# A list scheduler inside a kernel gets a corrected table of durations, and its small VectorE copies become bitwise or operations

## The chip, the cores and the metric

The kernel runs on one core of a Trainium2 chip. The metric is the device time of one launch in microseconds (us). A core has TensorE (matmuls, results in PSUM), VectorE, ScalarE, GpSimd and SyncE (it issues most DMAs), each with an instruction queue of its own that runs in order. In the profile they are PE (with PEld for the loading of weights), DVE, ACT, POOL and SP.

## The reference

A gated linear attention is followed by a Fourier mixing over tokens and features and by a feed-forward block, for 4 batches, 8 heads of 48 features, and 768 tokens (all float32):

```python
for t in range(S):
    state = alpha[:, :, t, :, None] * state + np.einsum('bhd,bhe->bhde', k[:, :, t], v[:, :, t])
    y[:, :, t] = np.einsum('bhd,bhde->bhe', q[:, :, t], state)
...
X = np.fft.fft(np.fft.fft(x, axis=1), axis=2)      # x: y as [4, 768, 384]
u = x + np.real(X)
un = (u - mean(u)) / np.sqrt(var(u) + 1e-06)
out = u + np.maximum(un @ w_ch1, 0.0) @ w_ch2      # 384 -> 1536 -> 384
```

## The kernel before

Heads are taken in pairs (112 partitions), so each batch has four pairs, 16 in all. For one pair, `products` makes the running products of the decays: two VectorE scans over 768 steps (tiles `w` and `al`, with a helper row `d`), and around them small copies of every 64th element. Products of k and q with these (`times`, on VectorE or GpSimd) give operands of TensorE; the score blocks are evacuated from PSUM by ScalarE and masked by GpSimd (`affine_select`); a short scan per head (`tt`, 288 elements) carries the state between blocks of 128 steps. From the eighth pair on the scores are made from split operands (`qs`). `combine` adds and subtracts the two halves of the sequence (tiles `sd`, mostly on GpSimd). `mix_stages` then folds the features (`f2`, VectorE, with three small copies for each of three tiles), multiplies by cosine and sine tables, and adds the result to `y`. `norm_stages` normalises, and `ffn_stages` runs the feed-forward block for each of two blocks of 384 tokens: 12 tiles of the hidden layer, each with 9 matmuls in and 9 out, because weights and activations are kept as a high and a low part. Between the two, ScalarE and VectorE make the high and low part of `h`. The weights arrive as float64 and are taken apart in `wsplit`, in the first part of the run.

None of this is emitted in program order. Every instruction is written down in a `Plan` with a key (a priority: numbers such as `KW`, `KN`, `KA`), the tiles it touches and an estimate of its duration (`duration`). `emit` then goes through time as it estimates it: it keeps a clock for every engine, asks which instructions have all their operands, takes the one with the lowest key among those that could start within a short window, gives it a tile, and advances the clock of its engine. The order so found is the order of the instructions in each engine's queue, DMA issues on SyncE and GpSimd included. Where an instruction may run on one of two engines (`FX`: `'VG'` is VectorE or GpSimd), this is where the engine is chosen:

```python
done = max(now, t) + op.durs[e] - SLACK[e]
if any(max(clock[o], start(op, o)) + op.durs[o] < done for o in op.engines if o != e):
    continue
```

The feed-forward block of one batch has a late key, so that it fills TensorE's time beside the attention of the next batch. The first 120 us of the plan get small matmuls on a tile of zeros wherever the plan sees TensorE idle (`WARM`). Since all instructions are emitted from `emit` (line 434), nearly all rows of the profile name that line; they are told apart by their tiles.

Of the kernel before, what the change touches and what calls it, by code (L numbers as in the profile page):

```python
# [112 lines left out]


class View:
    """A tile of the plan, or a part of one: the steps are replayed on the real tile."""

    def __init__(self, tile, steps=()):
        self.tile, self.steps = tile, steps
# [14 lines left out]


class Slot:
    """One tile as the program sees it; it gets a real tile of its tag when its first instruction is placed."""

    def __init__(self, tag, real=None):
        self.tag, self.real, self.uses, self.touched, self.access, self.last = tag, real, 0, [], [], None  # L140
# [1 line left out]


class Rows:
    """Row numbers of an indirect DMA."""

    def __init__(self, view):
        self.view = view
# [25 lines left out]


class Plan:
    """Instructions written down in program order, then given an order on every engine by list scheduling."""

    def __init__(self, engines):
        self.engines, self.ops, self.tags, self.direct, self.key, self.chain, self.fill = engines, [], {}, None, 0.0, None, False  # L180
# [35 lines left out]
    def add(self, engines, name, args, kwargs):  # L216
        engine = engines[0]
        fns = {e: self.method(e, name) for e in engines}
        if self.direct:
            return fns[engine](*[real(a) for a in args], **{k: real(x) for k, x in kwargs.items()})  # L220
        op = Op(engines, fns, args, kwargs, self.key)
        n = len(self.ops)
        self.ops.append(op)
        named = [("out" if i == 0 and "out" not in kwargs else i, a) for i, a in enumerate(args)] + list(kwargs.items())
        op.free, op.fill = 1, self.fill
        op.bytes = None
        for k, a in named:
            if isinstance(a, Rows):
                a = a.view
            if isinstance(a, View):  # L230
                self.touch(n, op, a, k in ("out", "accum_out"))
                if k == "out":
                    op.free = self.region(a)[4]
                if k == 2:
                    op.moving = a
        op.name = name
        named = dict((str(k), a) for k, a in named)
        op.durs = {e: self.duration(op, named, e) for e in engines}
        if engine == "SP" and isinstance(named["out"], View):
            if self.chain is not None and self.chain not in op.deps:  # L240
                op.behind = self.chain
                op.deps.add(self.chain)
            self.chain = n
        if "dma" in name:
            op.wire = self.wire(named)
# [43 lines left out]
    def duration(self, op, named, engine):  # L289
        n = op.free  # L290
        if "dma" in op.name:
            return 1.05 if engine == "POOL" else 0.05
        if engine == "PE":
            m = self.region(named["1"])[4]
            if op.name == "transpose":
                return max(m, self.region(named["2"])[4]) / 1200 + 0.002
            if str(named["1"].real(self.base(named["1"])).dtype).endswith("float32"):
                return max(m, n) / 600 + 0.004
            return n / 2400 + 0.003
        if engine == "ACT":  # L300
            pointer = 0.094 if any(isinstance(named.get(k), View) for k in ("bias", "scale")) else 0.0
            return (0.05 if self.psum(named.get("1")) else 0.093) + n / 1200 + pointer + (0.096 if "accum_out" in named else 0.0)
        if op.name == "memset":
            return n / (960 if engine == "DVE" else 1100) + 0.01
        if engine == "DVE":
            if op.name == "bn_stats":
                return 0.47
            if op.name == "reciprocal":
                return 0.07 + n / 160
            if isinstance(named.get("scalar1"), View):  # L310
                return 0.07 + n / 1200
            whole = "bitcast" in [s[0] for s in named.get("out", View(None)).steps]
            pointer = 0.06 if isinstance(named.get("scalar"), View) else 0.0
            return 0.07 + pointer + n / (1920 if whole and op.name == "tensor_scalar" else 960)
        return 0.126 + n / 1094 if op.name == "affine_select" else 0.15 + n / 477

    def psum(self, view):
        return isinstance(view, View) and view.tile.tag in ("a", "f1", "f2")
# [12 lines left out]
    def emit(self):  # L331
# [10 lines left out]
                    wait[e].append(n)  # L342
        dge, wire = 0.0, 0.0
        order = []

        def start(op, e):
            t = op.ready[e]
# [13 lines left out]
        while placed < len(ops):  # L361
# [38 lines left out]
                    order.append(self.idle[0])  # L400
            if op.name == "matmul" and self.idle and (op.args[0].tile.tag, op.args[0].tile.cell) == self.idle[3]:
                self.open = not op.kwargs["stop"]
            end = t + op.dur
            clock[op.engine] = end
            if "dma" in op.name:
# [38 lines left out]


SLACK = {'ACT': 2.0, 'DVE': 0.5, 'POOL': 5.0}
FX = {'comb': 'G', 'mul': 'VG', 'first': 'G', 'wm': 'VG', 'wd': 'VG', 'fold': 'V', 'ev': 'A', 'relu': 'A', 'un': 'V', 'hi': 'A', 'xh': 'A', 'er': 'AV', 'fc': 'V', 'kl': 'V'}
WINDOW = {'PE': 0.0, 'ACT': 0.15, 'DVE': 0.05, 'POOL': 0.5, 'SP': 0.0, 'DMA': 0.0}


# [1 line left out]
def gla_mix_ffn(ctx: ExitStack, tc: tile.TileContext, alpha, kq, v, w1, w2, consts, rowtab, out):  # L452
# [41 lines left out]
    def w3():  # L494
        return plan.tile("w3")

    def fixed(shape, name, dtype=F32):
        return plan.fixed(cp.tile(shape, dtype, name=name))

# [1 line left out]
    cst = fixed([P, CONST_W], "cst")  # L501
    ident = cst[:, ID_O : ID_O + P]
    wts = [None] * (NW // 2)
# [101 lines left out]
        FL["hi"].copy(hi, a2)  # L605
        FL["wd"].tensor_sub(lo, a2, hi.bitcast(F32))

# [1 line left out]
    def attn_stages(b, hp, i, mixed):  # L609
        tt, mt = tts[i], mts[hp % 3]  # L610
        pair = b * NP2 + hp
# [3 lines left out]
        def products(lo, hi):  # L615
            as_, Af, o = loaded["al", pair], e["A"], off(lo)
            d, chunks = d1[0:CW, lo:hi], slice(lo // C, hi // C)
            V.tensor_copy(d[:, 0::C], as_[0:CW, o : o + hi - lo : C])
            V.memset(as_[0:CW, o : o + hi - lo + 1 : C], 0.0)
            part = Af[0:CW, lo:hi]  # L620
            V.tensor_tensor_scan(out=part, data0=as_[0:CW, o : o + hi - lo], data1=d, initial=0.0, op0=ALU.mult, op1=ALU.add)
            V.memset(d[:, 0::C], 0.0)
            V.memset(d[:, C - 1 :: 2 * C], 1.0)
            r = rec[0:CW, chunks]
            V.reciprocal(r, part[:, C - 1 :: C])
            V.tensor_copy(d[:, 2 * C - 1 :: 2 * C], r[:, 1::2])
            j0, j1 = max(lo // P - 1, 0), hi // P - 1
            V.tensor_mul(mt[0:CW, j0:j1], Af[0:CW, j0 * P + P - 1 : j1 * P : P], Af[0:CW, j0 * P + P + C - 1 : j1 * P + C : P])
            V.tensor_tensor_scan(
                out=as_[0:CW, o + hi - lo : o : -1], data0=as_[0:CW, o + hi - lo : o : -1], data1=d[:, ::-1],  # L630
                initial=0.0, op0=ALU.mult, op1=ALU.add,
            )
            V.memset(d[:, C - 1 :: C], 0.0)
            first = part.rearrange(halves, h=2, t=C)[:, :, 0]
            FL["first"].tensor_mul(first, first, r[:, 0::2, None].broadcast_to([CW, (hi - lo) // P, C]))
# [119 lines left out]

        return [s1, s2, s3, s4, s5 if pair < FR else s5r, s6, s7, lambda: combine(*mixed(), hp * 2 * D, 2 * D, FL["comb"])]

# [1 line left out]
    def early():  # L759
        return plan.tile("x").bitcast(F32) if state["start"] else w3()  # L760

# [21 lines left out]
    def mix_stages(ytiles, zt, scr, us):  # L783
# [15 lines left out]
        def f2():  # L799
# [4 lines left out]
            for z, f in zip(zp, fp):  # L804
                ze, zo = f[:, :, 0 : HM + 1], f[:, :, HM:DM]
                E.tensor_add(ze[:, :, 1:HM], z[:, :, 1:HM], z[:, :, DM - 1 : HM : -1])
                FL["fc"].copy(ze[:, :, 0 : HM + 1 : HM], z[:, :, 0 : HM + 1 : HM])
                E.tensor_sub(zo[:, :, 1:HM], z[:, :, 1:HM], z[:, :, DM - 1 : HM : -1])
                g = [z[:, :, o : o + len(r)] for o, (r, _) in zip((0, HQ + 1, 2 * HQ + 1, 3 * HQ), GROUPS)]
                E.tensor_add(g[0][:, :, 0:HQ], ze[:, :, 0:HQ], ze[:, :, HM:HQ:-1])  # L810
                FL["fc"].copy(g[0][:, :, HQ : HQ + 1], ze[:, :, HQ : HQ + 1])
                E.tensor_sub(g[1][:, :, 0:HQ], ze[:, :, 0:HQ], ze[:, :, HM:HQ:-1])
                E.tensor_sub(g[2][:, :, 0 : HQ - 1], zo[:, :, 1:HQ], zo[:, :, HM - 1 : HQ : -1])
                E.tensor_add(g[3][:, :, 0 : HQ - 1], zo[:, :, 1:HQ], zo[:, :, HM - 1 : HQ : -1])
                FL["fc"].copy(g[3][:, :, HQ - 1 : HQ], zo[:, :, HQ : HQ + 1])
                for i in range(2):
                    e["zg"].append([x[:, i] for x in g])
            e["rt"] = []
# [63 lines left out]

        return [f0, f2, mk_s(0), mk_s(1), mk_s(2), mk_s(3), mk_d(0), mk_d(1), mk_d(2), fb]

# [1 line left out]
    def norm_stages(us, blk, res):  # L886
        e = {}

# [40 lines left out]

        return [n1, n2]  # L930

# [1 line left out]
    def ffn_stages(us, blk, res, store, f0=0, f1=DFF // P):  # L933
        e = {"h": {}}

# [163 lines left out]
        plan.idle = (lambda: nc.tensor.matmul(warm[2][0:32, 480:512], zero.real(), zero.real(), start=True, stop=True), 1.0, WARM, ("f2", 2))  # L1099
    with tc.manual_schedule():  # L1100
        plan.emit()
# [1 line left out]
    main_pool.close()  # L1103
    pp = ctx.enter_context(tc.tile_pool(name="fp", bufs=1, space=bass.MemoryType.PSUM))
    uid = [0]
# [97 lines left out]


def layout(q, k, v, alpha, moe_w_ch1, moe_w_ch2):
    """The inputs as the launch takes them: heads in pairs with the features before the tokens, float64 as 8-byte words."""

    def pairs(x, fill):
        t = np.full((B * NP2, CW, S), fill, np.float32)
# [14 lines left out]


def tokens(o):
    """The blocks of the launch as the rows of the sequence: the second block holds the tokens from the end."""
    res = np.empty((B, S, DM), o.dtype)
    res[:, 0:DM] = o[:, 0].reshape(B, DM, DM)
    res[:, row_table().T] = o[:, 1]  # L1230
    return res
# [16 lines left out]
```

## Time and profile before

| | |
|---|---|
| timed runs | 597.63, 600.06, 600.74 us (median 600.06) |
| span of the profiled execution, first to last instruction | 600.8 us |
| instructions | 9105 |
| mean granted TensorE clock | 0.887 |
| TensorE busy | 543.5 us |
| VectorE busy | 397.0 us |
| ScalarE, GpSimd busy | 213.4 us, 214.1 us |
| HBM read, written | 34.42 MB, 7.08 MB |

The profile shows one execution. Its span stands 0.7 us above the median of the timed runs. Busy times are sums over the engine's instructions; the granted clock is the share of its full clock that TensorE was given, so that the same matmul is longer where this is low. "Idle before, and its releaser" is the time in which an engine waited ahead of an instruction, and what ended it. A name such as `tt` stands for all tiles of that name. VectorE rows overlap a little, because an instruction starts before the one ahead of it has written its last result.

### The profile page before, as it was taken

How to read it: one execution, taken by the hardware profiler on the slowest of the kernel's cores; microseconds unless marked ns; L12 is line 12 of the kernel's file. 1: busy time of each engine (PE TensorE's matmuls, PEld its weight loads, DVE VectorE, ACT ScalarE, POOL GpSimd, SP SyncE). 2: the span in 40 equal slices, each digit the busy share in tenths (PEclk: the TensorE clock that was granted, in tenths of full speed). 3: DMA queues.
4: the chain of work that ended last, by engine and by line, in shares of the span. 5: the costliest groups of instructions: out<-in, count | busy, mean ns of one | idle time of the engine just before them, and what ended most of it. 6: DMA issues, size and time to landing. Idle time of an engine off the chain costs nothing. (4 is left out here: it accounts for less than half of the span.)

```text
span 600.8 us, 9105 instructions
## 1 busy us (share of the span) xinstructions
PE 543.5 (90%) x3470; PEld 523.2 (87%) x3470; DVE 397.0 (66%) x863; ACT 213.4 (36%) x442; POOL 214.1 (36%) x252
## 2 busy tenths in 40 slices
PE   7989588998779999787999989977999999999995
PEld 6878578897679998777999979977999999999995
DVE  7998999879955699896635991596635921412211
ACT  2657233575333313464622221444712121211110
POOL 3689794337526101395540040085740000000000
PEclk7568567689959999997979999987979999999999
DMA  8827291720014101143240110120010000100101
GB/s 219 280 74 278 67 321 50 247 67 0 2 35 130 48 0 41 44 130 92 67 140 6 40 47 0 41 67 21 1 55 26 33 8 1 40 1 1 40 1 44
DMA packets 16546, 42.16 MB, mean 70 GB/s; under 512 B 1904, under 2 KB 7088, under 8 KB 16496
## 3 DMA queue, kind: packets, MB, share of 16 engines
q1 hardware_dynamic: 15440, 39.08, 20.5%
q0 software_dynamic: 768, 2.36, 1.5%
q8 instruction: 29, 0.48, 0.4%
q14 instruction: 21, 0.17, 0.1%
q10 hardware_dynamic: 288, 0.07, 0.1%
HBM read 34.42 MB, written 7.08 MB: 69 GB/s over the span
## 5 line engine op out<-in xcount | busy, mean ns | idle before, releaser
L434 PE MATMUL f<-wt,h 128*128 128x384 f32 x864 | 179.5, 347 | 6.3 <-DVE h L434 3.3
L434 PE MATMUL f<-x,wt 128*128 128x384 f32 x864 | 179.7, 347 | 0.0
L434 PEld LDWEIGHTS f<-wt,h 128*128 128x128 f32 x864 | 154.2, 193 | 8.7 <-DVE h L434 4.5
L434 PEld LDWEIGHTS f<-x,wt 128*128 128x128 f32 x864 | 155.3, 193 | 0.6 <-issue 0.3
L434 DVE SCALAR_TENSOR_TENSOR h<-f,h 128x384 fp32r<-128x384 f32 x96 | 53.1, 553 | 128.9 <-ACT h L212 128.5
L212 ACT ACTIVATE h<-f 128x384 fp32r<-128x384 f32 x96 | 47.1, 491 | 192.4 <-PE f L434 181.4
L434 POOL TENSOR_SCALAR_AFFINE_SELECT w<-w 128x512 f32<-128x512 f32 (+1 forms) x64 | 48.8, 790 | 47.8 <-ACT w L434 47.8
L434 PEld LDWEIGHTS a<-vn,w 128*128 128x128 f32 x324 | 58.3, 251 | 7.4 <-POOL w L434 7.0
L434 PE MATMUL a<-vn,w 128*128 128x64 f32 x324 | 59.7, 326 | 5.4 <-POOL w L434 5.4
L434 POOL TENSOR_TENSOR sd<-y,y 128x288 f32<-128x288 f32 x32 | 30.8, 984 | 53.5 <-ACT y L434 52.3
L434 POOL TENSOR_TENSOR w<-w,rec 112x384 f32<-112x384 f32 (+1 forms) x17 | 17.8, 1049 | 87.2 <-DVE mt L434 83.2
L434 PE MATMUL a<-tt,w 112*128 112x96 f32 x134 | 40.5, 400 | 8.6 <-DVE tt L434 8.6
L434 DVE SCALAR_TENSOR_TENSOR qs<-w,hm,qs 112x384 fp32r<-112x384 f32 x36 | 24.7, 711 | 27.2 <-ACT qs L434 27.1
L434 ACT COPY w<-a 128x512 f32<-128x512 f32 (+6 forms) x58 | 25.9, 481 | 33.0 <-PE a L434 26.6
L434 DVE TENSOR_TENSOR_SCAN al<-al,d 112x768 f32<-112x768 f32 (+1 forms) x17 | 36.7, 2160 | 0.4
L434 DVE TENSOR_TENSOR y<-y,a 128x191 f32<-128x191 f32 (+2 forms) x96 | 28.7, 342 | 12.4 <-PE a L434 12.3
L434 PEld LDWEIGHTS a<-tt,w 112*128 112x128 f32 x134 | 28.0, 261 | 9.8 <-DVE tt L434 9.7
L434 PE MATMUL a<-qs,qs 112*128 112x256 f32 x162 | 31.6, 322 | 4.8 <-DVE qs L434 4.1
L434 POOL TENSOR_TENSOR w<-sd 128x96 f32<-128x96 f32 x64 | 35.7, 577 | 0.0
L434 PE MATMUL a<-cst,w 96*128 96x96 f32 (+10 forms) x267 | 33.7, 269 | 0.0
L434 PEld LDWEIGHTS a<-cst,w 128*96 128x96 f32 (+7 forms) x267 | 32.3, 169 | 0.9
L434 PEld LDWEIGHTS a<-qs,qs 112*128 112x128 f32 x162 | 26.1, 217 | 7.8 <-DVE qs L434 5.5
(124 smaller groups left out, 743.3 us busy)
## 6 DMA issues: line engine op xcount, KB each, us to landing
kq<-in_kq_dram SPq DMA_DIRECT2D x15, 672.0 KB, 7.5
wt<-in_w_dram SPq DMA_DIRECT2D x8, 768.0 KB, 9.6
al<-in_alpha_dram SPq DMA_DIRECT2D x15, 336.0 KB, 4.3
vn<-in_v_dram SPq DMA_DIRECT2D x16, 296.0 KB, 2.8
out_dram<-y SPq DMA_DIRECT2D x24, 192.0 KB, 1.9
wt<-in_w_dram SPq DMA_DIRECT2D x8, 384.0 KB, 6.3
scr<-y SPq DMA_DIRECT2D x4, 576.0 KB, 4.5
cst<-in_consts_dram SPq DMA_DIRECT2D x1, 832.5 KB, 5.2
```

The costliest lines, as they stand in the source:

```text
L212: return lambda out, x: e.activation(out, x, AF.Relu)
L434: op.ins = op.fns[op.engine](*[real(a) for a in op.args], **{k: real(x) for k, x in op.kwargs.items()})
```

## The change

The table in `duration` gets other constants, among them one for scans, one for operands with a stride above 16 bytes, and larger fixed parts for ScalarE. A new function `port` marks instructions of VectorE and GpSimd that use both SBUF operands or a wide copy; in `emit` an overlap of such instructions on the two engines lengthens the later one by half of the overlap (`SHARE`), or by all of it for the kind `"whole"`, and it moves GpSimd's clock when the later one is VectorE's. Five small copies in the source (66 of the instructions of the feature fold and of the whole-row decay products, and the four of the first pair) become `same`: a `tensor_tensor` that computes x or x on the bits, as int32, on VectorE, where the copies ran too. Keys, tiles and the arithmetic are otherwise as before. The diff, without removed comments:

```diff
@@ Plan.add
         op.durs = {e: self.duration(op, named, e) for e in engines}
+        op.port = self.port(op, named) if engine in ("DVE", "POOL") else None
@@ Plan.duration
             if str(named["1"].real(self.base(named["1"])).dtype).endswith("float32"):
-                return max(m, n) / 600 + 0.004
-            return n / 2400 + 0.003
+                slow = 1.65 if self.stride(named["2"]) > 16 else 1.0
+                return max(m, slow * n) / 600 + 0.004
+            return n / 2240 + 0.003
         if engine == "ACT":
             pointer = 0.094 if any(isinstance(named.get(k), View) for k in ("bias", "scale")) else 0.0
-            return (0.05 if self.psum(named.get("1")) else 0.093) + n / 1200 + pointer + (0.096 if "accum_out" in named else 0.0)
+            slow = 1.8 if self.stride(named["out"]) > 16 and n > 64 else 1.0
+            return (0.11 if self.psum(named.get("1")) else 0.14) + slow * n / 1200 + pointer + (0.25 if "accum_out" in named else 0.0)
...
+            if op.name == "tensor_tensor_scan":
+                return 0.1 + n / 480
             if isinstance(named.get("scalar1"), View):
-                return 0.07 + n / 1200
+                return 0.09 + n / 1200
             whole = "bitcast" in [s[0] for s in named.get("out", View(None)).steps]
             pointer = 0.06 if isinstance(named.get("scalar"), View) else 0.0
-            return 0.07 + pointer + n / (1920 if whole and op.name == "tensor_scalar" else 960)
+            return 0.09 + pointer + n / (1920 if whole and op.name == "tensor_scalar" else 960)
+    def port(self, op, named):
+        if op.engine == "POOL":
+            return None if "dma" in op.name else "part"
+        if op.engine != "DVE" or op.name == "memset":
+            return None
+        inputs = [a for k, a in named.items() if k != "out" and isinstance(a, View)]
+        wide = [a for a in inputs if a.tile.tag not in ("a", "f1", "f2") and self.region(a)[4] > 1]
+        if len(wide) > 1:
+            return "part"
+        return "whole" if wide and op.name in ("tensor_scalar", "tensor_copy", "copy") and "scalar1" in named else None
@@ Plan.emit
+        held = {"DVE": (0.0, 0.0), "POOL": (0.0, 0.0)}
...
+            if op.port and op.engine in held:
+                other = "POOL" if op.engine == "DVE" else "DVE"
+                a, b = held[other]
+                both = max(0.0, min(b, t + op.dur) - max(a, t))
+                op.dur += (SHARE if op.port == "part" else 1.0) * both
+                if other == "POOL":
+                    clock[other] += SHARE * both
+                held[op.engine] = (t, t + op.dur)
             end = t + op.dur
@@ gla_mix_ffn
+SHARE = 0.5
+    def same(out, x):
+        x = x.bitcast(I32)
+        V.tensor_tensor(out=out.bitcast(I32), in0=x, in1=x, op=ALU.bitwise_or)
-            V.tensor_copy(d[:, 0::C], as_[0:CW, o : o + hi - lo : C])
+            same(d[:, 0::C], as_[0:CW, o : o + hi - lo : C])
-            V.tensor_copy(d[:, 2 * C - 1 :: 2 * C], r[:, 1::2])
+            same(d[:, 2 * C - 1 :: 2 * C], r[:, 1::2])
-                FL["fc"].copy(ze[:, :, 0 : HM + 1 : HM], z[:, :, 0 : HM + 1 : HM])
+                same(ze[:, :, 0 : HM + 1 : HM], z[:, :, 0 : HM + 1 : HM])
-                FL["fc"].copy(g[0][:, :, HQ : HQ + 1], ze[:, :, HQ : HQ + 1])
+                same(g[0][:, :, HQ : HQ + 1], ze[:, :, HQ : HQ + 1])
-                FL["fc"].copy(g[3][:, :, HQ - 1 : HQ], zo[:, :, HQ : HQ + 1])
+                same(g[3][:, :, HQ - 1 : HQ], zo[:, :, HQ : HQ + 1])
```

More of the change, by code (lines that the diff above doesn't have):

```diff
@@ L309, in duration, with stride @@
                 return 0.07 + n / 160
+            if op.name == "tensor_tensor_scan":
+                return 0.1 + n / 480
             if isinstance(named.get("scalar1"), View):
-                return 0.07 + n / 1200
+                return 0.09 + n / 1200
             whole = "bitcast" in [s[0] for s in named.get("out", View(None)).steps]
             pointer = 0.06 if isinstance(named.get("scalar"), View) else 0.0
-            return 0.07 + pointer + n / (1920 if whole and op.name == "tensor_scalar" else 960)
+            return 0.09 + pointer + n / (1920 if whole and op.name == "tensor_scalar" else 960)
         return 0.126 + n / 1094 if op.name == "affine_select" else 0.15 + n / 477
+    def stride(self, view):
+        ap = view.real(self.base(view))
+        return abs(ap.ap[-1][0]) * mybir.dt.size(ap.dtype)
+    def port(self, op, named):
[8 more added lines that the diff above has]
+        return "whole" if wide and op.name in ("tensor_scalar", "tensor_copy", "copy") and "scalar1" in named else None
     def psum(self, view):
@@ L446 @@
 SLACK = {'ACT': 2.0, 'DVE': 0.5, 'POOL': 5.0}
-FX = {'comb': 'G', 'mul': 'VG', 'first': 'G', 'wm': 'VG', 'wd': 'VG', 'fold': 'V', 'ev': 'A', 'relu': 'A', 'un': 'V', 'hi': 'A', 'xh': 'A', 'er': 'AV', 'fc': 'V', 'kl': 'V'}
+FX = {'comb': 'G', 'mul': 'VG', 'first': 'G', 'wm': 'VG', 'wd': 'VG', 'fold': 'V', 'ev': 'A', 'relu': 'A', 'un': 'V', 'hi': 'A', 'xh': 'A', 'er': 'AV', 'kl': 'V'}
+SHARE = 0.5
 WINDOW = {'PE': 0.0, 'ACT': 0.15, 'DVE': 0.05, 'POOL': 0.5, 'SP': 0.0, 'DMA': 0.0}
```

## The prediction

> **What bounds the kernel now.** I read the busy times and the stretches first, then the chain that ended last, then the groups of TensorE and VectorE by line, the order of time around TensorE's long waits, and last the instructions that stand beside each other on VectorE and GpSimd. The span is 600.8 us against a median of 600.06 us of the timed runs; the sum below is made against 600.8 and 0.7 is taken off at the end.
>
> ```profile
> PE 543.5 (90%) x3470; PEld 523.2 (87%) x3470; DVE 397.0 (66%) x863; ACT 213.4 (36%) x442; POOL 214.1 (36%) x252
> ...
> PE 26%; DVE 0%; issue 0%
> ```
> ```profile
> 0.00:105.00 105.00, 85.88 (x681) 79.20 (x682) 95.69 (x184) 47.12 (x94) 73.43 (x77) 0.67 0.60 184
> 105.00:300.00 195.00, 173.28 (x1086) 164.78 (x1085) 157.02 (x332) 90.50 (x183) 85.70 (x104) 0.90 0.22 70
> 300.00:420.00 120.00, 111.11 (x668) 108.07 (x668) 77.80 (x184) 36.44 (x81) 35.39 (x39) 0.92 0.15 45
> 420.00:470.00 50.00, 48.98 (x326) 47.83 (x325) 27.34 (x72) 17.74 (x39) 19.54 (x34) 0.92 0.08 25
> ```
> The columns after the stretch are TensorE, weight load, VectorE, ScalarE and GpSimd in us, then the granted clock. There are two regimes. Up to 105 us there is no feed-forward work yet, VectorE is busy 95.69 of 105 us, and it sets the pace. From 105 us TensorE does. Up to 470 us it stands idle for 21.7 + 8.9 + 1.0 = 31.6 us, and its mean clock is only 0.90 to 0.92.
>
> The last 123 us show whether those idle times could be filled (matmuls of the weight tiles alone):
> ```profile
> 470.00:593.00 123.00, 122.21 (x691) 1.00 0.04 15
> ```
> One batch has 2 blocks x 12 tiles x 18 = 432 feed-forward matmuls, so 691 after 470 us means that at least 259 of an earlier batch are left when the attention is over, 46 us of work at 122.21/691 = 0.177 us each. In the second half TensorE thus had other work ready in principle while it waited, and it waited because the written order put something else first. That order is what the changed table makes.
>
> **The change part by part.**
>
> *Copies that become bitwise or.* The instructions concerned are these; the last row is no copy, but the nearest instruction of the new kind, with two inputs in SBUF and few elements.
> ```profile
> L434 DVE COPY d<-al 112x12 f32<-112x12 f32 x15 | 8.1, 538 | 0.2
> L434 DVE COPY w<-x 128x2 f32<-128x2 f32 x6 | 5.8, 975 | 0.0
> L434 DVE COPY d<-rec 112x6 f32<-112x6 f32 x15 | 4.1, 275 | 0.1
> L434 DVE COPY w<-w 128x2 f32<-128x2 f32 x18 | 2.9, 162 | 0.0
> L434 DVE COPY w<-w 128x4 f32<-128x4 f32 x9 | 1.5, 200 | 2.9 <-POOL w L434 1.7 <-issue 1.1
> L434 DVE COPY x<-w 128x4 f32<-128x4 f32 x3 | 1.1, 430 | 0.0
> L434 DVE TENSOR_TENSOR mt<-w 112x5 f32<-112x5 f32 x15 | 3.9, 260 | 0.0
> ```
> 66 copies take 23.5 us; at the undisturbed 162 ns they would take 10.7, so 12.8 us is waiting. Three collisions show for what:
> ```profile
> 38.78 3.87 POOL L434 TENSOR_TENSOR w<-kq,w 112x768 f32<-112x768 f32 x1
> 40.89 1.79 DVE L434 COPY d<-al 112x12 f32<-112x12 f32 x1
> ...
> 87.05 5.07 DVE L434 COPY w<-x 128x2 f32<-128x2 f32 x1
> 87.60 0.84 POOL L434 TENSOR_TENSOR w<-w,rec 112x384 f32<-112x384 f32 x1
> 88.39 1.93 POOL L434 TENSOR_SCALAR_AFFINE_SELECT w<-w 128x384 f32<-128x384 f32 x4
> 90.29 1.79 POOL L434 TENSOR_TENSOR w<-kq,w 112x768 f32<-112x768 f32 x1
> ...
> 161.81 1.81 POOL L434 TENSOR_TENSOR w<-w,w 128x768 f32<-128x768 f32 x1 [2.54 <-DVE w L434]
> 162.29 1.36 DVE L434 TENSOR_TENSOR mt<-w 112x5 f32<-112x5 f32 x1
> ```
> The first copy ends at 42.68, just after GpSimd's instruction ends at 42.65. The second ends at 92.12, after a run of GpSimd instructions that ends at 92.08: it sat out six of them. The third row pair is the warning: a two-input instruction of 5 elements also waited, to 163.65, for a GpSimd instruction that ended at 163.62. So an or still waits for the GpSimd instruction in flight; no two-input row of this trace waits through a whole run of them. Bounds for the gain: 0 (an or waits exactly as a copy does) and 12.8 us (it never waits). By the nearest row, the third pair, the long wait of the second copy would end with its first GpSimd instruction, at 88.44 instead of 92.08, and the others stay: I take 3.6 us. It lies in the first 105 us, where VectorE sets the pace, so all of it counts. Copies later than 105 us I cost at nothing: they have the feed-forward work beside them.
>
> The Trainium skill (SBUF — State Buffer, Who interferes with whom) says that a VectorE instruction with two SBUF inputs contends with a GpSimd instruction that reads SBUF, and that the loser fully blocks for the whole instruction. The third pair agrees (1.36 us for 5 elements). By this rule alone the edit would bring 0 us instead of 3.6.
>
> *The table of durations.* Nothing in it runs on the chip; it changes the order. What it was wrong about:
> ```profile
> L434 DVE TENSOR_TENSOR_SCAN al<-al,d 112x768 f32<-112x768 f32 x15 | 34.6, 2304 | 0.4
> L434 DVE TENSOR_TENSOR_SCAN w<-al,d 112x768 f32<-112x768 f32 x15 | 28.9, 1928 | 0.3
> L434 DVE TENSOR_TENSOR_SCAN tt<-us,seg 48x288 f32<-48x288 f32 x16 | 16.5, 1033 | 0.5
> L434 DVE TENSOR_TENSOR_SCAN tt<-us,seg 64x288 f32<-64x288 f32 x16 | 14.5, 906 | 0.0
> ```
> The old formula gives 0.07 + 768/960 = 0.87 us and 0.37 us for these; the new one 0.1 + 768/480 = 1.70 and 0.70. The feed-forward matmul goes from 0.163 to 0.174 planned (0.177 measured above). The plan so learns that VectorE's part of the attention is late, by 30 x 0.83 + 32 x 0.33 = 35 us over the kernel, more than TensorE's 1728 x 0.011 = 19 us, and it will put feed-forward matmuls ahead of matmuls that need a scan.
>
> What that is worth is read from TensorE's waits for the scans (first three rows) and the clock behind them:
> ```profile
> 168.97 0.79 PE L434 MATMUL a<-cst,al 112*128 112x112 f32 x3 [6.51 <-DVE al L434]
> 276.31 0.59 PE L434 MATMUL a<-tt,w 112*128 112x96 f32 x2 [3.33 <-DVE tt L434]
> 413.34 0.59 PE L434 MATMUL a<-tt,w 112*128 112x96 f32 x2 [2.83 <-DVE tt L434]
> 359.58 2.61 PE L434 MATMUL f<-wt,h 128*128 128x384 f32 x7 [2.25 <-DVE al L434]
> 400.24 0.70 PE L434 MATMUL a<-qs,qs 112*128 112x256 f32 x2 [2.90 <-DVE qs L434]
> ```
> ```profile
> 165.00:180.00 15.00, 11.03 (x51) 11.06 (x52) 9.14 (x13) 5.11 (x12) 4.43 (x7) 0.50 0.10 28
> 276.00:282.00 6.00, 5.69 (x30) 5.69 (x31) 2.37 (x6) 1.99 (x5) 0.81 (x2) 0.62 0.13 25
> 413.00:420.00 7.00, 6.66 (x33) 6.66 (x34) 2.77 (x5) 2.68 (x7) 1.48 (x2) 0.57 0.15 43
> ```
> The three waits are 12.7 us. Behind each the granted clock falls, and TensorE's busy time there costs 11.03 x 0.50 + 5.69 x 0.38 + 6.66 x 0.43 = 10.5 us more than at full clock. Together 23.2 us hang on three misjudged scans. How much of it the new table sees, I take from the chain in front of the second:
> ```profile
> 271.27 2.38 DVE L434 TENSOR_TENSOR_SCAN al<-al,d 112x768 f32<-112x768 f32 x1
> 273.58 0.72 DVE L434 TENSOR_TENSOR_SCAN tt<-us,seg 64x288 f32<-64x288 f32 x1
> 274.36 1.90 DVE L434 TENSOR_TENSOR_SCAN tt<-us,seg 48x288 f32<-48x288 f32 x1
> ```
> It took 4.99 us (271.27 to 276.26); the old table has 1.61, the new one 3.10 before the port's share. That closes 1.49 of 3.38, 44%: 10.2 us. The other two waits, 5.2 us, are no scans; I leave them. Late next, where a scan is no longer waited for, is ScalarE's evacuation and VectorE's part of it.
>
> *The port's share, ScalarE's table and the rest.* They put each overlap of VectorE and GpSimd at half its length on the plan and add some 0.05 us to each ScalarE instruction. Where this moves an instruction no row shows. Bounds: a gain of the 5.2 us above, and a loss as in the third rival; I take 0. TensorE's warm-up matmuls are placed by the plan's idle time; they run in TensorE's gaps, 19.1 us up to 105 us, and are costed at nothing for that. The DMA issues keep their bytes; in the plan's order loads stand two pairs ahead, and that lead covers them. The indirect DMAs stay on GpSimd's queue among its other work.
>
> Sum: 600.8 - 3.6 - 10.2 = 587.0, less 0.7: 586.3 us, put at 586.
>
> **The rivals.**
>
> 1. *The or waits like the copy.* For it: the pair at 162 us, and the skill's rule above. Against: no two-input row waits through several GpSimd instructions. Time: 586 + 3.6 = 590.
>
> 2. *The waits move.* Of TensorE's 31.6 us of idle time only 12.7 are the three waits behind scans, the rest is spread over many; a new order can lose elsewhere what it wins here, since affine selects, evacuations and VectorE's 157.02 of 195 us are still tight between 105 and 300 us. Then only the copies remain: 600.8 - 3.6 - 0.7 = 596.5.
>
> 3. *GpSimd becomes late (slower).* The multiplications by k and q may run on VectorE or GpSimd, and the plan picks by which is done sooner.
> ```profile
> L434 POOL TENSOR_TENSOR al<-kq,al 112x768 f32<-112x768 f32 x8 | 14.4, 1804 | 14.4 <-DVE al L434 14.4
> L434 DVE TENSOR_TENSOR al<-kq,al 112x768 f32<-112x768 f32 x7 | 7.7, 1094 | 0.2
> 67.20 1.54 PE L434 MATMUL f<-vn,w 128*128 128x64 f32 x6 [6.43 <-POOL w L434]
> ```
> With scans charged double, VectorE looks late and more of them go to GpSimd. Each moved one stands 1.80 us ahead of the affine selects and sums queued there, for which TensorE already waits up to 6.43 us. In the first 105 us GpSimd passes VectorE from (95.69 - 73.43)/(1.80 + 1.09) = 7.7 moved ones on. If all the delay is on the path, 8 moved ones (14.4 us) eat the 13.8 us gained; 12 give 586.3 + 21.6 = 608. Against it: the port's share also makes GpSimd look later, which holds such work on VectorE.
>
> 4. *Nearly all waits go:* the five long waits and their clock (17.8 + 10.5) and the copies' 3.6: 600.8 - 31.9 - 0.7 = 568.
>
> **How the numbers follow.** The forecast has 0.33, the first rival 0.15, the second 0.22, the third 0.22, the fourth 0.08. About 0.5% (3 us) is what the measurement tells from no change, so 597 to 603 counts as the same. The second rival straddles that bound: 0.08 of it falls below, 0.14 inside. Faster: 0.33 + 0.15 + 0.08 + 0.08 = 0.64; same 0.14; slower 0.22. The likeliest case alone reaches from 576 (the 12.8 us of the copies) to 595 (a third of the gain). The range that leaves 2 in 10 out, half of the third rival and most of the fourth, is 570 to 607.
>
> **What would show it.** Right: no small VectorE instruction above 2 us in the first 105 us; TensorE's waits for scan outputs below 1 us each, its idle time from 105 us on near 25 us, and granted clocks above 0.92 there. Wrong on the copies: small or instructions of several us beside GpSimd runs. Third rival: more than 8 of the multiplications newly on GpSimd, and TensorE's waits for GpSimd above 15 us. Second rival: the scan waits gone, and as much idle time before other matmuls. What would make the forecast wrong is above all an order that is worse for reasons the table doesn't hold.

## The result and the profile after

The changed kernel takes 577.92 us (median of 575.28 to 580.21) against 600.4 us of the kernel before in the same comparison: a ratio of 0.962, 95% interval 0.958 to 0.966. The forecast was 586 us in a range of 570 to 607. Where medians of the kernel before differ in the experiments below (598.99 to 601.37 us), each ratio is against the runs of its own comparison. Some runs were disturbed and the ratios leave them out; of the kernel with scans planned too short the profiled run is one of them.

From the page of the changed kernel, the busy times, and from the view by stretches the same columns as before (TensorE, weight load, VectorE, ScalarE, GpSimd, then the clock):

```profile
PE 537.3 (93%) x3836; PEld 515.2 (89%) x3836; DVE 401.7 (69%) x864; ACT 213.0 (37%) x444; POOL 216.0 (37%) x249
```
```profile
0.00:105.00 105.00, 92.09 (x1008) 84.29 (x1008) 87.13 (x180) 47.51 (x93) 65.76 (x74) 0.75 0.61 185
105.00:300.00 195.00, 176.93 (x1130) 167.74 (x1131) 163.99 (x328) 85.75 (x175) 87.97 (x94) 0.93 0.21 65
300.00:420.00 120.00, 116.81 (x790) 113.44 (x790) 92.27 (x205) 51.20 (x117) 51.38 (x65) 1.00 0.18 54
420.00:470.00 50.00, 49.50 (x326) 48.53 (x326) 32.90 (x105) 11.57 (x27) 10.86 (x18) 1.00 0.11 37
```
VectorE, ScalarE and GpSimd are as busy as they were. What changed is TensorE between 105 and 470 us: idle for 18.1 + 3.2 + 0.5 = 21.8 us instead of 31.6, and with a clock of 0.93, 1.00 and 1.00 instead of 0.90, 0.92 and 0.92. The first of these clocks tells little: an execution in the old order, with the or operations, had 0.93, 0.94 and 0.93. From 105 us to the end of the span TensorE is idle for 28.3 us instead of 38.2 and busy for 445.2 us instead of 457.6, so of the 22.3 us by which the span is shorter 9.9 are idle time and 12.4 busy time.

Two landmarks show where the time went: ScalarE's first evacuation of the hidden layer (the feed-forward work begins) and the last matmuls with `tt` (the attention ends). Of the kernel before:

```profile
123.14 0.49 ACT L212 ACTIVATE h<-f 128x384 fp32r<-128x384 f32 x1
...
442.17 0.69 PE L434 MATMUL a<-tt,w 112*128 112x96 f32 x2
```
and of the changed kernel:

```profile
131.36 0.49 ACT L212 ACTIVATE h<-f 128x384 fp32r<-128x384 f32 x1 [1.46 <-PE f L465]
...
427.88 0.54 PE L465 MATMUL a<-tt,w 112*128 112x96 f32 x2
```
The first part became 8.2 us longer. The stretch between the landmarks went from 319.0 to 296.5 us, 22.5 us shorter, and what follows from 158.6 (to the span of 600.8) to 150.6 us (to 578.5), 8.0 us shorter. The gain is all in the part where TensorE sets the pace.

The waits of TensorE of 2 us or more in the changed kernel (idle time and what ended it in brackets):

```profile
78.17 0.56 PE L465 MATMUL f<-cst,w 128*97 128x65 f32 x2 [7.05 <-issue]
106.05 2.18 PE L465 MATMUL a<-vn,kt 128*112 128x96 f32 x10 [2.75 <-DVE y L465]
114.93 0.82 PE L465 MATMUL a<-cst,al 112*128 112x112 f32 x3 [4.28 <-POOL al L465]
289.75 1.44 PE L465 MATMUL a<-qs,qs 112*128 112x256 f32 x5 [3.05 <-DVE d L465]
```
The three waits for scans on which the prediction rested (6.51, 3.33 and 2.83 us) are gone, and so are the two others it listed. Between 131 and 428 us one wait of that size is left. The slow clock goes with the waits, as the stretch right behind that one shows beside one with no wait:

```profile
289.00:295.00 6.00, 5.25 (x24) 5.24 (x24) 4.83 (x13) 3.10 (x7) 1.05 (x2) 0.50 0.01 1
413.00:420.00 7.00, 7.00 (x56) 6.99 (x55) 2.85 (x5) 5.41 (x14) 3.82 (x8) 1.00 0.00 0
```
A wait need not be long for that. In the kernel before, one of 0.92 us for a scan, which the prediction did not list, is followed by 6 us at 0.50 too:

```profile
437.32 0.59 PE L434 MATMUL a<-tt,w 112*128 112x96 f32 x2 [0.92 <-DVE tt L434]
```
```profile
438.00:444.00 6.00, 6.00 (x28) 6.00 (x28) 0.17 (x1) 0.80 (x2) 0.63 (x1) 0.50 0.00 0
```
Which waits cost the clock was not tried.

### The profile page after: what moved, and what is told of

Its sections match the earlier page's. It is cut to its first block, busy times and chain, and to the rows that moved or that the text cites. A ratio compares the mean times of both kernels' runs of the same rounds, so it can differ in the third digit from the quotient of the medians.

```text
span 578.5 us, 9801 instructions
## 1 busy us (share of the span) xinstructions
PE 537.3 (93%) x3836; PEld 515.2 (89%) x3836; DVE 401.7 (69%) x864; ACT 213.0 (37%) x444; POOL 216.0 (37%) x249
## 5 line engine op out<-in xcount | busy, mean ns | idle before, releaser
L465 PE MATMUL f<-wt,h 128*128 128x384 f32 x864 | 177.7, 344 | 2.4 <-DVE h L465 2.4
L465 PEld LDWEIGHTS f<-x,wt 128*128 128x128 f32 x864 | 151.3, 189 | 0.6 <-issue 0.2
L465 POOL TENSOR_SCALAR_AFFINE_SELECT w<-w 128x512 f32<-128x512 f32 (+1 forms) x64 | 52.5, 845 | 47.7 <-ACT w L465 47.6
L465 PEld LDWEIGHTS a<-vn,w 128*128 128x128 f32 x324 | 48.8, 209 | 4.9 <-POOL w L465 4.2
L465 PE MATMUL a<-vn,w 128*128 128x64 f32 x324 | 49.4, 282 | 3.0 <-POOL w L465 2.9
L465 POOL TENSOR_TENSOR sd<-y,y 128x288 f32<-128x288 f32 x32 | 31.5, 1004 | 38.2 <-ACT y L465 36.8
L465 DVE TENSOR_TENSOR_SCAN al<-al,d 112x768 f32<-112x768 f32 (+1 forms) x17 | 41.4, 2436 | 0.2
L465 PE MATMUL a<-tt,w 112*128 112x96 f32 x134 | 36.6, 367 | 1.1 <-DVE tt L465 1.0
L465 PE MATMUL a<-qs,qs 112*128 112x256 f32 x162 | 29.8, 297 | 5.3 <-DVE d L465 3.1
L465 DVE TENSOR_TENSOR_SCAN tt<-us,seg 64x288 f32<-64x288 f32 (+1 forms) x32 | 28.2, 881 | 9.3 <-ACT us L465 8.8
L1135 PEld LDWEIGHTS f<-zero 128*32 128x32 f32 x616 | 26.8, 129 | 6.5 <-issue 1.2
```

The source lines that it names most:

```text
L465: op.ins = op.fns[op.engine](*[real(a) for a in op.args], **{k: real(x) for k, x in op.kwargs.items()})
```

## The experiments

Theory A: the gain is the new order, which keeps TensorE from waiting for scans. Rivals: B, small copies held up by GpSimd; C, the port's term; D, the other constants; E, the warm-up matmuls; F, any new order.

**The or operations alone, and the order alone.** First, the kernel before with `same` instead of its copies:

```diff
-            V.tensor_copy(d[:, 0::C], as_[0:CW, o : o + hi - lo : C])
+            same(d[:, 0::C], as_[0:CW, o : o + hi - lo : C])
...
```


> The kernel before with the bitwise or operations alone; the table is the old one, and the order of every engine stays that of the kernel before. Theory A (the new order carries the gain): 597 to 600 us, at most the 3.6 us that the prediction gave the copies. Rival B (small copies held up by GpSimd were the loss): 585 us or less, most of the 22 us. An or waits for the GpSimd instruction in flight as a copy does, so the group d<-al stays near 540 ns by A and falls below 200 ns by B; the 5.07 us copy at 87 us should fall to about 1.4 us by A.

Measured: 600.72 us, ratio 0.9995 (0.9965 to 1.0025). The groups of this kernel, to be held against 538 and 975 ns of the copies:

```profile
L434 DVE TENSOR_TENSOR d<-al 112x12 int32<-112x12 int32 x15 | 8.1, 539 | 0.2
L434 DVE TENSOR_TENSOR w<-x 128x2 int32<-128x2 int32 x6 | 5.8, 972 | 0.0
```
The or operations last as long as the copies to within a few ns. So does the collision near 87 us, for which 1.4 us had been expected: the or takes the 5.07 us of the copy and ends at 92.55, where GpSimd's run ends at 92.53.

```profile
87.48 5.07 DVE L434 TENSOR_TENSOR w<-x 128x2 int32<-128x2 int32 x1
```
Then the reverse, the changed kernel with copies in the same order:

```diff
     def same(out, x):
-        x = x.bitcast(I32)
-        V.tensor_tensor(out=out.bitcast(I32), in0=x, in1=x, op=ALU.bitwise_or)
+        V.tensor_copy(out, x)
...
-        if len(wide) > 1:
+        if len(wide) > 1 or op.name == "tensor_copy":
             return "part"
```


> The changed kernel with the small copies put back, planned as if they were the or operations, so that the order of every engine is that of the changed kernel. Theory A: 578 to 582 us. Rival B: 595 us or more.

Measured: 577.47 us, ratio 0.962 (0.957 to 0.966), the same as the changed kernel. In both orders this half of the change is worth nothing that can be measured. B is out.

**The port's term and the durations, each without the other.**

```diff
-        op.port = self.port(op, named) if engine in ("DVE", "POOL") else None
+        op.port = None
```


> The changed kernel without the term for the shared port in the plan; corrected durations and or operations stay. Theory A (the durations of the scans and of the other instructions carry it): 578 to 585 us. Rival C (the port's term carries it, since the overlap of VectorE and GpSimd is what the plan missed): 593 us or more, near the kernel before.

Measured: 586.11 us, ratio 0.976 (0.971 to 0.980): 15.3 us faster than the kernel before, a little slower than A expected. TensorE's idle time between 105 and 470 us is as low here as in the changed kernel (21.1 and 21.8 us). But by 105 us it has run only 394 matmuls besides the warm-up ones, against 436, and from there on it is busy for 455.0 us, against 445.2. The next kernel keeps `port` and the code in `emit`, and has the old body of `duration` throughout:

```diff
-            if op.name == "tensor_tensor_scan":
-                return 0.1 + n / 480
...
-            return n / 2240 + 0.003
+            return n / 2400 + 0.003
```


> The changed kernel with the old table of durations and the port's term kept. Theory A: 592 to 602 us, near the kernel before. Rival C: 578 to 584 us. If both this and the kernel without the port's term come out between, each part carries a share.

Measured: 592.27 us, ratio 0.986 (0.981 to 0.990): 9.1 us faster, at the lower edge of what A expected. The two parts add up to 24.4 us, against 22.9 that the whole change brings in that comparison's terms (0.0381 x 601.37). So C holds beside A: each part is a cause by itself. That the port's is the smaller one is less sure, since each size comes from one order.

**The scans alone, and all but the scans.**

```diff
+            if op.name == "tensor_tensor_scan":
+                return 0.1 + n / 480
```


> The kernel before with one line of the new table alone: a scan is planned as 0.1 + n/480. Theory A (TensorE's waits were misjudged scans, as the prediction has it): 587 to 592 us, most of the 15 us that the corrected durations gave without the port's term, and no wait for a scan's output above 2 us after 105 us. Rival D (the rest of the table, above all TensorE's and ScalarE's constants, does it): 597 us or more.

Measured: 592.5 us, ratio 0.993 (0.987 to 0.998): 4.4 us by the ratio, less than A expected. From 105 us on the profile puts no wait of 2 us or more down to a scan; these are left:

```profile
143.45 0.93 PE L436 MATMUL a<-w,al 48*128 48x128 f32 x6 [2.12 <-DVE x L436]
172.94 0.42 PE L436 MATMUL a<-cst,al 112*128 112x112 f32 x1 [3.07 <-issue]
358.99 1.33 PE L436 MATMUL f<-wt,h 128*128 128x384 f32 x6 [2.33 <-DVE h L436]
```
The one of 3.07 us is what remains of the longest wait before (6.51 us at 168.97): it starts 0.10 us after the end of the product `al` (172.84), which had to wait for a scan beside GpSimd at work:

```profile
167.88 3.83 DVE L436 TENSOR_TENSOR_SCAN al<-al,d 112x768 f32<-112x768 f32 x1
```
All in all TensorE's idle time between 105 and 470 us is down to 22.4 us, nearly that of the changed kernel. What is not down is its busy time from 105 us on: 455.0 us, against 457.6 before and 445.2 in the changed kernel. By 105 us it has run 411 matmuls besides the warm-up ones, against 436 there; how much of the 10 us that explains was not followed.

The changed kernel without these two lines:

```diff
-            if op.name == "tensor_tensor_scan":
-                return 0.1 + n / 480
```


> The changed kernel without the line for scans; all other constants, the port's term and the or operations stay. Theory A: 588 us or more, and waits of 2 to 6 us for scan outputs come back. Rival D: 576 to 582 us.

Measured: 590.8 us (median of four runs, 586.57 to 592.62), ratio 0.989 (0.982 to 0.996), as A expected; D, with 576 to 582 us, is out as the whole cause. One wait for a scan is back, and others with it:

```profile
173.76 0.69 PE L463 MATMUL f<-wt,h 128*128 128x384 f32 x1 [3.44 <-DVE h L463]
393.85 0.60 PE L463 MATMUL a<-qs,qs 112*128 112x256 f32 x2 [2.07 <-DVE qs L463]
408.27 0.74 PE L463 MATMUL a<-tt,w 112*128 112x96 f32 x2 [3.20 <-DVE tt L463]
```
So the line for scans brings 0.7% as the first correction and 2.7% (0.989 to 0.962) as the last one. The other constants likewise: beside the port's term they bring nothing (0.986 and 0.989), beside the scan line 1.7% (0.993 to 0.976). Corrections of a plan are not terms of a sum: what one is worth depends on which others are made. The other constants alone, and the scan line with the port's term alone, were not run.

**The warm-up matmuls.** The new plan sees longer idle times on TensorE and emits 616 rows of them instead of 250. In the changed kernel spaced as follows, 234 rows are left:

```diff
-DUMMY = 0.11
+DUMMY = 0.27
```


> The changed kernel with its warm-up matmuls spaced 0.27 us instead of 0.11 us in the plan, so that about as many run as in the kernel before (250 rows instead of 616); the order of all other instructions is unchanged. Theory A (the order carries the gain): 576 to 581 us. Rival E (the plan's longer idle times give more warm-up matmuls, and the clock of 0.75 instead of 0.67 up to 105 us is the gain): 584 us or more, with the clock there back near 0.67.

Measured: 578.4 us, ratio 0.969 (0.964 to 0.974). And in the kernel before:

```diff
-DUMMY = 0.11
+DUMMY = 0.045
```


> The kernel before with its warm-up matmuls spaced 0.045 us in the plan, so that some 600 rows run; nothing else is changed. Theory A: 598 to 603 us. Rival E: 594 us or less, with a higher clock up to 105 us.

Measured: 600.74 us, ratio 1.006 (1.000 to 1.012). The first 105 us of the two:

```profile
0.00:105.00 105.00, 81.63 (x656) 74.27 (x656) 87.30 (x182) 47.35 (x93) 67.09 (x74) 0.80 0.59 184
```
```profile
0.00:105.00 105.00, 87.43 (x1023) 81.30 (x1024) 92.38 (x176) 46.53 (x93) 70.48 (x76) 0.80 0.61 185
```
With 650 rows the kernel before has a clock of 0.80 there instead of 0.67 and is no faster; with fewer of them the changed kernel's clock did not fall either. E is out: up to 105 us TensorE's clock is not what counts (by the two ratios, 0.962 and 0.969, the extra ones bring 0.7% at most, within the intervals).

**Scans planned too short, and planned as measured.**

```diff
-                return 0.1 + n / 480
+                return 0.07 + n / 1920
```


> The changed kernel with scans planned too short on purpose: 0.07 + n/1920, 0.47 us for 768 elements, half of the old estimate. Theory A (the error in the scans' durations is what costs): slower than the kernel without the scan line, 594 us or more, with longer waits for scan outputs. Rival F (any new order of this plan comes out near 580 to 592, whatever it believes of the scans): 592 us or less.

Measured: ratio 1.010 (1.002 to 1.019), 602.19 to 609.07 us. From its profile only the place of the waits is read, here those for scans from 105 us on:

```profile
179.44 0.74 PE L465 MATMUL a<-tt,w 112*128 112x96 f32 x2 [5.45 <-DVE tt L465]
291.70 0.60 PE L465 MATMUL a<-tt,w 112*128 112x96 f32 x2 [4.40 <-DVE tt L465]
427.01 0.74 PE L465 MATMUL a<-tt,w 112*128 112x96 f32 x2 [4.57 <-DVE tt L465]
```
With every other correction in place, one wrong line costs all of the gain and brings back three waits for scans. F in its plain form is out: not any new order is good.

```diff
-                return 0.1 + n / 480
+                return 0.1 + n / 364
```


> The changed kernel with scans planned as the trace has them on the mean: 0.1 + n/364, 2.21 us for 768 elements and 0.89 for 288. Theory A: 570 to 578 us, a little faster than the changed kernel. Rival F: anywhere between 575 and 592 us.

Measured: 583.27 us, ratio 0.977 (0.970 to 0.983). Here A missed: the measured mean is a worse entry than 0.1 + n/480. A measured scan holds its waits for GpSimd, which the port's term charges again; but why the time went this way is open. The feed-forward work began late, which does not explain it: in the kernel with both edits below it began at 140.26, and nothing was lost:

```profile
139.84 0.49 ACT L212 ACTIVATE h<-f 128x384 fp32r<-128x384 f32 x1 [0.55 <-PE f L465]
```

```diff
-SHARE = 0.5
+SHARE = 1.0
```


> The changed kernel with an overlap of VectorE and GpSimd charged in full instead of by half, as the rows show that the one waits for the other's whole instruction. Theory A with the port's term as a second cause: 570 to 579 us. Rival F: 580 us or more.

Measured: 575.51 us, ratio 0.961 (0.954 to 0.968), the same as the changed kernel.

Then both of these edits together:

```diff
-                return 0.1 + n / 480
+                return 0.1 + n / 364
...
-SHARE = 0.5
+SHARE = 1.0
```


> Both of these: scans at 0.1 + n/364 and overlaps in full. Since the measured duration of a scan already holds its waits for GpSimd, this counts them twice. Theory A: 572 to 582 us, not better than either alone. Rival F: anywhere between 575 and 592 us.

Measured: 578.07 us, ratio 0.966 (0.960 to 0.971), also the same. The double counting does not show as a loss here, so it alone does not explain the kernel above. F keeps this much: among plans that are about right, 575 to 583 us is a matter of which order happens to come out, and no version tried is clearly better than the change. A spread of nearly 8 us between such plans also means that the 4.4 and 9.1 us of single parts above are sizes of one order each.

## Why the prediction was right, and where it was not

Of the 14.4 us that the forecast took off, 3.6 brought nothing, so that it came as near as it did is partly luck: without them it would have said 590. The direction and the cause were right.

*The direction and the place.* TensorE's waits behind misjudged scans were the cause named, and the three are gone: over the whole run its waits for `tt` fell from 8.6 to 2.1 us and those for VectorE's `al` from 11.0 to 1.1. The argument that feed-forward matmuls were there to fill them held: 46 us of them were left over before, and the attention now ends 14.3 us earlier with as much VectorE work done.

*The size of the table's term* was too small: 10.2 us forecast, 15.3 us measured for the durations. The step that failed is that it was worked out from scans alone, by the 44% of the lateness that their line closes in one chain, with the rest of the table at 0. The scan line by itself brought 4.4 us; it left 3.07 of the 6.51 us of the longest wait, which is near such a share. With the other constants beside it no wait behind a scan was longer than 1.57 us from 105 us on, and the clock between 300 and 470 us was 0.99 to 1.00. So the constants of other instructions, put at 0 in the sum, count as well.

*The port's share* was costed at 0 and is worth 9.1 us by itself. The prediction bounded it with the 5.2 us of the two waits that are no scans, and chose 0 because no row showed where the term would move an instruction. The rows were there, in the chain ahead of the longest wait; the first row is a scan with GpSimd idle:

```profile
93.57 1.72 DVE L434 TENSOR_TENSOR_SCAN w<-al,d 112x768 f32<-112x768 f32 x1
...
157.49 3.39 DVE L434 TENSOR_TENSOR_SCAN w<-al,d 112x768 f32<-112x768 f32 x1
...
163.76 3.82 DVE L434 TENSOR_TENSOR_SCAN al<-al,d 112x768 f32<-112x768 f32 x1
```
The two scans of that chain, each with GpSimd at work beside it, take 3.8 us more than two undisturbed ones, which no constant for a scan can tell the plan. With the port's term alone the waits of 6.51 and 3.33 us are gone.

*The copies* were given 3.6 us and brought 0. The step that failed is the bound from one pair of rows: since a two-input instruction had been seen to wait for one GpSimd instruction, none was thought to wait through several. The scan at 163.76 above already spoke against it: it lost 2.1 us, and the GpSimd instruction in flight when it began ended 0.8 us later (164.56), with others behind it. In the changed kernel an or of 2 elements does wait so:

```profile
80.94 4.18 DVE L465 TENSOR_TENSOR w<-x 128x2 int32<-128x2 int32 x1
...
81.00 0.85 POOL L465 TENSOR_TENSOR w<-w,rec 112x384 f32<-112x384 f32 x1
81.79 1.56 POOL L465 TENSOR_TENSOR al<-kq,al 112x768 f32<-112x768 f32 x1
83.29 1.81 POOL L465 TENSOR_TENSOR w<-kq,w 112x768 f32<-112x768 f32 x1
```
It ends at 85.12, the last of the three at 85.10. This was the first rival's mechanism (0.15). It is also the rule of the Trainium skill (SBUF — State Buffer, Who interferes with whom) that a VectorE instruction with two SBUF inputs contends with a GpSimd instruction that reads SBUF. The trace agrees, with 4.18 us for 2 elements here and 539 ns for the or against 538 for the copy. The Trainium skill (SBUF — State Buffer, SBUF: two separate sides) has the second to start block while the first has the ports, for a whole instruction; here the wait spans three.

*The first 105 us* were thought to be shortened; they did not end sooner, and the feed-forward work began 8.2 us later.

*The third rival* did not come: GpSimd has 14 of the multiplications by k and q, one of them of half a row, against 15 before.

```profile
L465 POOL TENSOR_TENSOR w<-kq,w 112x768 f32<-112x768 f32 x7 | 18.8, 2680 | 0.4
L465 POOL TENSOR_TENSOR al<-kq,al 112x768 f32<-112x768 f32 x6 | 9.6, 1602 | 0.0
L465 POOL TENSOR_TENSOR w<-kq,w 112x384 f32<-112x384 f32 x1 | 1.2, 1188 | 0.1
```
Nor did the second: TensorE's idle time did not stay where it was.

Of what would show the forecast right, the idle time (21.8 us, near 25 said) and the clocks (0.93 to 1.00, above 0.92 said) came; that no small VectorE instruction would pass 2 us did not. From 105 us on waits for scan outputs stayed under 1 us but for one: the wait of 3.05 us at 289.75 stands behind a scan (last section), though the profile names `d`.

## What to carry to other kernels

Where a written order feeds in-order queues, look for idle time of the bounding engine while other work for it is left over: that time is an error of the plan, and its durations can be checked against the profile's groups one by one. Correct them together, since what one correction brings depends on the others (0.7% or 2.7% for the same line here), and include what engines take from each other. To replace an instruction in order to free it from a shared port, first find rows of the new kind under the same contention, large instructions too, and look at the longest case, not at one.

## What was not expected of the hardware

A VectorE instruction with two SBUF inputs can be held through a long run of GpSimd instructions, the large ones too. The longest case in the changed kernel is a scan of 768 steps that took 5.99 us, where one with GpSimd idle beside it took 1.76 (first row); it ends 1.6 us after a run of nine GpSimd instructions (282.78 to 287.63):

```profile
87.06 1.76 DVE L465 TENSOR_TENSOR_SCAN w<-al,d 112x768 f32<-112x768 f32 x1
...
283.25 5.99 DVE L465 TENSOR_TENSOR_SCAN al<-al,d 112x768 f32<-112x768 f32 x1
...
282.78 1.25 POOL L465 TENSOR_TENSOR w<-w,rec 112x384 f32<-112x384 f32 x1 [0.75 <-DVE mt L465]
...
287.24 0.39 POOL L465 TENSOR_TENSOR w<-sd,w 128x96 f32<-128x96 f32 x1
```
It is also what stands behind the one wait of 3.05 us that is left at 289.75: the matmul's `qs` is made from this scan's output and is done at 289.70. Other two-input instructions got through after one GpSimd instruction (the pair at 162 us of the kernel before). There GpSimd's next instruction began 0.11 us after the first had ended (163.73), while in the run of nine each began before the one ahead had ended. Whether that decides was not tried and stays open.
